# Placing the second halves of the value products on other columns of TensorE, in an attention and expert kernel

## The chip, the core and the metric

The program runs on one core of one Trainium2 chip, as one launch. The metric is the time of that launch on the device, in microseconds (us). Engines: TensorE (PE in the profile, PEld its weight loads), VectorE (DVE), ScalarE (ACT), GpSimd (POOL) and SyncE (SP), which issues the transfers. The engines run their own instruction streams in order and wait for each other on semaphores.

## What is computed

Attention over 4 batches of 12 heads (448 positions, 64 values each) with a soft cap on the scores, then a hidden layer with a squared ReLU, then a soft mixture of eight experts. Everything is float32.

```python
def _attn_ref(q, k, v, cap):                       # (4, 12, 448, 64)
    scores = cap * np.tanh(np.matmul(q, k.transpose(0, 1, 3, 2)) / np.sqrt(64) / cap)
    attn = np.exp(scores - np.max(scores, axis=-1, keepdims=True))
    attn = attn / (np.sum(attn, axis=-1, keepdims=True) + 1e-09)
    return np.matmul(attn, v)

def _moe_ref(x, w_in, w_out, s, b):                # 1792 tokens, 768 -> 2048 -> 768
    r = np.maximum(x @ w_in, 0.0)
    return (s * (r * r) + b) @ w_out

def _moe2_ref(x, phi, w1, w2):                     # 8 experts, 4 slots each
    ...
    d = softmax over tokens of x @ phi;  slot_input = d.T @ x
    for e in range(8): slot_out[e] = np.maximum(slot_input[e] @ w1[e], 0.0) @ w2[e]
    return softmax over slots of (x @ phi) @ slot_out
```

## The kernel before

**Groups, pairs, chunks.** The 48 heads are taken in twelve groups Q = 0 to 11 of four heads, three groups to a batch. A group is two pairs of heads (p = 2Q and 2Q+1), and i = 0 to 3 counts the heads of a group. The 448 key positions are cut in three chunks of 128 and a rest of 64 (c or k = 0 to 3, `KF` = 3 is the rest). Keys lie on the partitions of a score tile and queries along its free side. In a full chunk every head has a tile of 128 partitions. In the rest the two heads of a pair share one tile: the even head has partitions 0 to 63, the odd head 64 to 127 (`rows`, L186).

**Per group.** `scores` (L138) or, from Q = 6 on, `visit` (L162) makes the products of keys and queries, ScalarE takes tanh (L156, L158, L171, L180) and `expo` (L210) the exponential. `add` (L222) sums the chunks on VectorE into `es`, and `sums` (L232) sums `es` over the partitions with ones on TensorE; for Q < 3 the rests go straight into that sum (L240). ScalarE and VectorE then make its reciprocal `rec` (L243, L244).

**The value products.** `weighted` (L246) multiplies the exponentials by the values. Head i's 64 value columns are taken as two halves h of 32, so that each product uses 32 columns of TensorE and all four heads stand side by side in its 128 columns. The result `U` is one PSUM tile of 128 partitions and two banks; bank h holds half h, and head i has partitions 32i to 32i+31 in both. A chunk is therefore eight products of 448 columns: half 0 of heads 0 to 3, then half 1 of heads 0 to 3. In the rest a product has only 64 of the 128 rows of TensorE. Each float32 product is two weight loads and two matmuls in the trace. For Q < 3 the chunks are multiplied one by one; for Q = 3 to 5 chunks 0 and 1 together and later chunk 2 and the rest; from Q = 6 all 32 products in a row.

**The end of a group.** `finish` (L262) multiplies U by `rec` (L271), splits the outcome into a high part (L92, on ScalarE from Q = 2 on) and a low part (L93, on VectorE), and writes both into the tile x of the batch, whose layout `w_in` follows. U has one buffer, so that the next group's value products, and from Q = 6 on the second score tile of its first visit, wait until U has been read.

**The hidden layer.** For batch bi, `hidden` (L529) makes 16 blocks of 18 products (`hp`, L541) from x and the split `w_in` (`ws`, L525 and L526), then squares (L547, L548), and `post` and `chain` work the outcome into logits and slot inputs. Batch 0's block runs beside groups 3 to 5, batch 1's beside 6 to 8, batch 2's beside 9 to 11, batch 3's alone. Up to about the middle of the program VectorE and ScalarE also convert the weights from 64-bit patterns (`convert`, L388 to L421; results `wr` and `o`), which transfers bring in as `raw`. At the end 54 tiles of expert weights of 1 MB (`wt`) are streamed in for `tail`.

**The order.** A scheduler places the instructions of every engine from the program order, priorities and its own estimates of time, so that a change in one place can move instructions elsewhere. After it each engine runs its list in that order.

## Time and profile before

| | us |
|---|---|
| three runs | 620.32, 623.55, 622.86; median 622.86 |
| the profiled execution | 623.18 |
| its span, first to last instruction | 621.3 |
| TensorE busy | 573.0 |
| ScalarE busy | 400.4 |
| VectorE busy | 376.3 |
| TensorE clock granted, mean | 0.99 of 2.4 GHz |

The profiled execution's own time is 1.9 us above its span and 0.3 us above the median. Busy time is the time in which an engine had at least one instruction under way; side by side matmuls count once. The chain of waits is followed back from the last instruction, at each step to what released it. Times within the program are us from the span's start.

### The profile page before, as it was taken

The page shows a single profiled execution, that of the slowest core. Times are in us where ns is not written, and L with a number is a line of the kernel's source. Part 1 is how long each engine was busy: PE and PEld are TensorE (multiplying, and loading weights), DVE is VectorE, ACT ScalarE, POOL GpSimd, SP SyncE. Part 2 cuts the span into 40 slices and gives each one's busy share as a digit, 9 for nine tenths or more (in the row PEclk, how much of TensorE's full clock was granted, in tenths as well). Part 3 has the DMA queues.
Part 4 walks back from the last instruction along what each step waited for, and adds up shares of the span by engine and source line. Part 5 has one row for each costly group of instructions (what it writes and reads, how often), then busy time and mean ns, then how long its engine had stood idle before and what let it go on. Part 6 is the DMA issues. An engine that isn't in the chain of part 4 may idle for free.

```text
span 621.3 us, 11132 instructions
## 1 busy us (share of the span) xinstructions
PE 573.0 (92%) x4496; PEld 383.7 (62%) x4496; DVE 376.3 (61%) x557; ACT 400.4 (64%) x675; POOL 4.1 (1%) x11
## 2 busy tenths in 40 slices
PE   7898999999989999999999999999999998986662
PEld 5334565757667576575875675858788864345551
DVE  4999999999984868868739845452422224112221
ACT  5899788888769698497797694945456551001010
POOL 1000000000000000000000000000000000000000
PEclk8999999999999999999999999999999999999996
DMA  8844767777684662859755322115878859999997
GB/s 295 289 133 140 242 247 250 251 239 280 190 294 168 221 206 77 277 181 297 244 186 163 123 69 80 52 51 207 325 296 298 330 198 407 419 419 418 417 411 267
DMA packets 44875, 149.97 MB, mean 241 GB/s; under 512 B 4480, under 2 KB 18576, under 8 KB 37904
## 3 DMA queue, kind: packets, MB, share of 16 engines
q1 hardware_dynamic: 44528, 148.65, 66.6%
q8 instruction: 37, 0.61, 0.4%
q0 software_dynamic: 288, 0.53, 0.2%
q14 instruction: 22, 0.18, 0.1%
HBM read 131.07 MB, written 18.09 MB: 240 GB/s over the span
## 4 chain that ended last, share of the span: by engine, by line
PE 59%; DMA 14%; ACT 13%; DVE 9%; issue 3%; SPq 0%; DVEq 0%; ACTq 0%
PE hp L541 30%; DMA wt<-in_w_dram 12%; PE U L257 9%; PE tp L564 4%; ACT e L218 3%; ACT e L180 3%; PE sc L146 2%; PE pt L654 2%; PE sc L176 2%; PE L L578 2%; PE Sm L238 2%; ACT e L156 1%; ACT g L566 1%; DMA raw<-in_w_outT_dram 1%; ACT ws L525 1%
## 5 line engine op out<-in xcount | busy, mean ns | idle before, releaser
L541 PE MATMUL hp<-x,ws 128*128 128x448 f32 x1152 | 267.6, 375 | 0.0
L541 PEld LDWEIGHTS hp<-x,ws 128*128 128x128 f32 x1152 | 207.2, 188 | 43.4 <-issue 28.7
L526 DVE TENSOR_TENSOR ws<-wr,ws 128x384 fp32r<-128x384 f32 x128 | 70.0, 551 | 93.6 <-ACT ws L525 92.6
L525 ACT CAST ws<-wr 128x384 fp32r<-128x384 f32 x128 | 67.5, 532 | 40.9 <-PE hp L541 40.6
L257 PE MATMUL U<-e,v 128*32 128x448 f32 (+1 forms) x672 | 70.4, 548 | 3.3 <-ACT e L218 2.5
L218 ACT ACTIVATE e<-e,c_acap 128x1792 f32<-128x1792 f32 (+1 forms) x42 | 72.0, 1713 | 0.3
L566 ACT COPY g<-tp 112x256 f32<-112x256 f32 x128 | 44.2, 404 | 12.3 <-PE tp L564 11.5
L257 PEld LDWEIGHTS U<-e,v 128*32 128x32 f32 (+1 forms) x672 | 20.0, 110 | 42.8 <-issue 35.5
L156 ACT ACTIVATE e<-sc,c_tsc 128x896 f32<-128x896 f32 x36 | 35.5, 1005 | 11.1 <-PE sc L146 11.1
L564 PE MATMUL tp<-c_cst,r 128*112 128x128 f32 x256 | 39.3, 275 | 3.2 <-ACT g L566 2.4
L244 DVE RECIPROCAL rec<-rec 128x448 f32<-128x448 f32 x12 | 35.4, 2949 | 9.8 <-ACT rec L243 9.8
L910 ACT COPY wt<-op 128x512 f32<-128x512 f32 x12 | 7.0, 586 | 52.4 <-PE op L905 52.4
L547 ACT ACTIVATE r<-hp 128x448 f32<-128x448 f32 x63 | 35.4, 563 | 7.8 <-PE hp L541 7.8
L180 ACT ACTIVATE e<-sc,c_tsc 128x896 f32<-128x896 f32 x36 | 35.6, 1050 | 5.2 <-PE sc L176 5.2
L925 PE MATMUL so_ps<-wt,free 128*32 128x128 f32 x768 | 25.9, 275 | 13.7 <-DMA wt<-in_w_dram 13.7
L548 ACT ACTIVATE r<-r 128x448 f32<-128x448 f32 x63 | 38.1, 605 | 0.4
L564 PEld LDWEIGHTS tp<-c_cst,r 128*112 128x112 f32 x256 | 29.6, 133 | 12.9 <-ACT g L566 4.6
L388 ACT ACTIVATE o<-raw 128x768 f32<-128x768 f32 x32 | 29.9, 949 | 5.3 <-DMA raw<-in_w_outT_dram 3.7
L227 DVE TENSOR_TENSOR es<-e 128x1792 f32<-128x1792 f32 x12 | 24.3, 2026 | 12.7 <-ACT e L218 12.7
L925 PEld LDWEIGHTS so_ps<-wt,free 128*32 128x32 f32 x768 | 19.9, 109 | 18.1 <-DMA wt<-in_w_dram 15.6
L417 DVE SCALAR_TENSOR_TENSOR o<-raw,o 128x768 int32<-128x768 int32 x32 | 30.5, 954 | 0.3
L421 DVE SCALAR_TENSOR_TENSOR o<-raw,o 128x768 int32<-128x768 int32 x32 | 30.4, 953 | 0.2
(177 smaller groups left out, 675.2 us busy)
## 6 DMA issues: line engine op xcount, KB each, us to landing
wt<-in_w_dram SPq DMA_DIRECT2D x48, 1024.0 KB, 18.0
wr<-wsc SPq DMA_DIRECT2D x48, 384.0 KB, 3.5
raw<-in_w_in_dram SPq DMA_DIRECT2D x16, 768.0 KB, 5.5
raw<-in_w_outT_dram SPq DMA_DIRECT2D x16, 768.0 KB, 5.1
raw<-in_w_out_dram SPq DMA_DIRECT2D x16, 768.0 KB, 5.9
wsc<-wr SPq DMA_DIRECT2D x16, 384.0 KB, 2.7
osc<-o SPq DMA_DIRECT2D x16, 384.0 KB, 3.5
wt<-osc SPq DMA_DIRECT2D x6, 1024.0 KB, 6.9
```

Of the source, the lines that this page charges most:

```text
L156: nc.scalar.activation(self.e[Q][c][:, 2 * j:2 * j + 2, :], sc[:, :, :S], AF.Tanh, scale=self.c["tsc"])
L180: nc.scalar.activation(self.e[Q][c][:, 2 * j:2 * j + 2, :], sc[j][:, :, :S], AF.Tanh, scale=self.c["tsc"])
L218: ins = self.nc.scalar.activation(e, e, AF.Exp, scale=self.c["acap"]).ins
L244: nc.vector.reciprocal(self.rec, self.rec)
L257: products.append(lambda k=k, h=h, i=i, d=d: nc.tensor.matmul(self.U[32 * i:32 * i + 32, h, :S], self.v[2 * Q + i // 2][self.rows(i, k), d ...
L525: self.nc.scalar.copy(hi, u)
L526: self.nc.vector.tensor_sub(lo, u, hi.bitcast(F32))
L541: nc.tensor.matmul(hp[:, :S], ws[kc // 3][:, w, kc % 3, :], x[:, s, kc, :], start=(k == 0), stop=(k == 3 * KC - 1))
L548: self.mark = nc.scalar.activation(r2, r2, AF.Square).ins
L564: self.nc.tensor.transpose(tp[:CP, q * P:(q + 1) * P], r2[:, q * CP:(q + 1) * CP], self.c["idn"])
L566: self.nc.scalar.copy(self.g[q][:CP, :, fc * P:(fc + 1) * P], tp[:CP, 2 * q * P:2 * (q + 1) * P].rearrange("p (a b) -> p a b", b=P))
L925: nc.tensor.matmul(so_ps[32 * e:32 * e + 32, G, :], ht[G][:, f, 32 * e:32 * e + 32], w2[f // 4][:, f % 4, e, :], start=(f == 0), stop=(f = ...
```

## The change

Five things, all of them about where a half of a head or a rest stands.

1. `weighted`: half 1 of head i goes to column strip i ^ 2, so the strips of the second half come in the order 2, 3, 0, 1. In bank 1 of U the heads stand in the order 2, 3, 0, 1.
2. `rows`: in the rests of the odd pairs the two heads swap rows, so that heads 0 and 3 of a group have rows 0 to 63 and heads 1 and 2 rows 64 to 127. With the first point the eight products of a rest are in eight different parts of TensorE, of 64 rows by 32 columns each; before, the two halves of a head shared one part. The key layout `kT` and the value layout `v` are made to fit on the host.
3. `add`: the two sums of the rests (L230) take heads 0 and 3, and 1 and 2.
4. `finish`: the one product of U and `rec` becomes three, 128 partitions by 448 for bank 0 and twice 64 partitions by 448 for bank 1, each with the other half of `rec`.
5. `w_in` is laid out on the host so that its rows follow the new order of x. Sizes and counts of transfers are as before.

```diff
--- before.py
+++ after.py
@@ -185,7 +185,7 @@
 
     def rows(self, g, c):
 
-        return slice(0, P) if c < KF else slice(64 * (g % 2), 64 * (g % 2) + 64)
+        return slice(0, P) if c < KF else slice(64 * ((g ^ g // 2) % 2), 64 * ((g ^ g // 2) % 2) + 64)
 
     def greatest(self, g):
         nc, c = self.nc, self.c
@@ -227,7 +227,8 @@
                 self.nc.vector.tensor_add(es, e[0] if c == 1 else es, e[c])
             for i in range(2) if c == KF else ():
                 r = self.rows(i, c)
-                self.nc.vector.tensor_add(es[r, i::2, :], es[r, i::2, :], e[c][r])
+                j = slice(1, 3) if i else slice(0, 4, 3)
+                self.nc.vector.tensor_add(es[r, j, :], es[r, j, :], e[c][r])
 
     def sums(self, Q):
 
@@ -254,8 +255,9 @@
             for h in range(2):
                 for i in range(4):
                     d = (i % 2 * KF + k if k < KF else 2 * KF) * D + 32 * h
-                    products.append(lambda k=k, h=h, i=i, d=d: nc.tensor.matmul(
-                        self.U[32 * i:32 * i + 32, h, :S], self.v[2 * Q + i // 2][self.rows(i, k), d:d + 32], self.chunk(4 * Q + i, k),
+                    j = 32 * (i ^ 2 * h)
+                    products.append(lambda k=k, h=h, i=i, j=j, d=d: nc.tensor.matmul(
+                        self.U[j:j + 32, h, :S], self.v[2 * Q + i // 2][self.rows(i, k), d:d + 32], self.chunk(4 * Q + i, k),
                         start=(k == 0), stop=(k == KF)))
         self.together(products, Q >= 3)
 
@@ -268,7 +270,9 @@
         u = self.U[:, :, :S]
         out = self.c["hh"][:, :, :S] if Q < 2 else u
         with self.tc.high_priority(100) if Q < NQ else nullcontext():
-            nc.vector.tensor_mul(out, u, self.rec[:, None, :].to_broadcast([P, 2, S]))
+            nc.vector.tensor_mul(out[:, 0], u[:, 0], self.rec)
+            for a, b in ((0, 64), (64, 0)):
+                nc.vector.tensor_mul(out[a:a + 64, 1], u[a:a + 64, 1], self.rec[b:b + 64])
             self.split(hi, lo, out, Q < 2)
         del self.e[Q], self.v[2 * Q], self.v[2 * Q + 1]
 
@@ -1011,14 +1015,19 @@
     kt = np.zeros((B * NP, 2, D, KW), np.float32)
     kt[..., :n] = kd[..., :n].reshape(B * NP, 2, D, P, KF).swapaxes(3, 4).reshape(B * NP, 2, D, n)
     for i in range(2):
-        kt[:, i, :, n + 64 * i:n + 64 * i + 64] = kd[:, i, :, n:]
+        for j in range(2):
+            r = n + 64 * (i ^ j)
+            kt[j::2, i, :, r:r + 64] = kd[j::2, i, :, n:]
     a["kT"] = kt.reshape(B * NP, P, KW)
-    a["v"] = cc(np.concatenate([vd[:, i, :n].reshape(B * NP, P, KF * D) for i in range(2)] + [vd[:, :, n:].reshape(B * NP, P, D)], axis=2))
+    vr = vd[:, :, n:].copy()
+    vr[1::2] = vr[1::2, ::-1]
+    a["v"] = cc(np.concatenate([vd[:, i, :n].reshape(B * NP, P, KF * D) for i in range(2)] + [vr.reshape(B * NP, P, D)], axis=2))
     wi, wo = cc(inputs["moe_w_in"]), cc(inputs["moe_w_out"])
     f64 = wi.dtype == np.float64
     if f64:
         wi, wo = wi.view(np.int64), wo.view(np.int64)
-    wi = wi.reshape(NQ, 4, 2, D // 2, FF).transpose(0, 2, 1, 3, 4)
+    wi = wi.reshape(NQ, 4, 2, D // 2, FF).transpose(0, 2, 1, 3, 4).copy()
+    wi[:, 1] = wi[:, 1][:, [2, 3, 0, 1]]
     a["w_in"] = cc(wi.reshape(KC, P, FC, P).transpose(2, 1, 0, 3)).reshape(FC, P, KC * P)
     a["w_outT"] = cc(wo.reshape(FF // U, U, 2, KC // 2, P).transpose(0, 2, 4, 3, 1)).reshape(FF // U, 2, P, CU)
     a["w_out"] = wo.reshape(FC, P, DM) if f64 else cc(wo.reshape(FC, P, 3, U).transpose(2, 1, 0, 3)).reshape(3, P, 4096)
```

The scheduler's lists change too. Three places follow; line numbers behind L235 are those of each version (L271 before is L273 and L275 after, L417 L421, L541 L545).

VectorE at the end of group 2, whose x is the last that batch 0's hidden layer waits for; `wr`, `o` and `ws` are weights under conversion, `ql` the low part of a query. Before:

```order
L244 RECIPROCAL rec<-rec 128x448
L479 COPY c_hh<-pf 128x64
L271 TENSOR_TENSOR U<-U,rec 128x2x448
L421 SCALAR_TENSOR_TENSOR wr<-raw,wr 128x768
L93 TENSOR_TENSOR ql<-q_648,qh 128x448
L93 TENSOR_TENSOR x_396<-U,x_396 128x896
```

After:

```order
L245 RECIPROCAL rec<-rec 128x448
L483 COPY c_hh<-pf 128x64
L273 TENSOR_TENSOR U<-U,rec 128x448
L425 SCALAR_TENSOR_TENSOR wr<-raw,wr 128x768
L275 TENSOR_TENSOR U<-U,rec 64x448
L93 TENSOR_TENSOR ql<-q_652,qh 128x448
L275 TENSOR_TENSOR U<-U,rec 64x448
L530 TENSOR_TENSOR ws<-wr,ws 128x384
L397 TENSOR_SCALAR o<-o 128x768
L421 SCALAR_TENSOR_TENSOR o<-raw,o 128x768
L93 TENSOR_TENSOR x_396<-U,x_396 128x896
```

The three parts of the product stand apart, and between the last of them and the low part of x three more instructions have come.

TensorE at the same place; the product that waits for ScalarE is the first that needs this x, and the one that waits for VectorE the first that needs its low part. Before:

```order
L541 MATMUL hp<-x_396,ws 128x448 x6
L146 MATMUL sc<-qh,kh 128x448 [waits Activation_49]
L146 MATMUL sc<-qh,kh 128x448
L146 MATMUL sc<-ql,kh 128x448 x2
L146 MATMUL sc<-qh,kl 128x448 x2
L541 MATMUL hp<-x_396,ws 128x448 [waits Activation_49]
L541 MATMUL hp<-x_396,ws 128x448 x3
L541 MATMUL hp<-x_396,ws 128x448 [waits DVE_49]
```

After:

```order
L545 MATMUL hp<-x_396,ws 128x448 x6
L146 MATMUL sc<-qh,kh 128x448 [waits Activation_49]
L146 MATMUL sc<-qh,kh 128x448
L146 MATMUL sc<-ql,kh 128x448 x2
L146 MATMUL sc<-qh,kl 128x448 x2
L545 MATMUL hp<-x_396,ws 128x448 [waits Activation_49]
L545 MATMUL hp<-x_396,ws 128x448 x3
L545 MATMUL hp<-x_396,ws 128x448 [waits DVE_49]
```

What stands ahead of the eight rows of after is another six `hp` products and six of scores, which in before came behind them; the first product that needs this x has moved back by those twelve.

VectorE from the first reading of U to the low part of x at the end of group 3, which frees U for group 4. Before:

```order
L271 TENSOR_TENSOR U<-U,rec 128x2x448
L526 TENSOR_TENSOR ws<-wr,ws 128x384
L393 TENSOR_SCALAR o<-o 128x768
L93 TENSOR_TENSOR ql<-q_982,qh 128x448
L417 SCALAR_TENSOR_TENSOR o<-raw,o 128x768
L93 TENSOR_TENSOR x_1051<-U,x_1051 128x896
```

After:

```order
L273 TENSOR_TENSOR U<-U,rec 128x448
L93 TENSOR_TENSOR kl<-k_989,kh 128x512
L530 TENSOR_TENSOR ws<-wr,ws 128x384
L275 TENSOR_TENSOR U<-U,rec 64x448
L397 TENSOR_SCALAR wr<-wr 128x768
L275 TENSOR_TENSOR U<-U,rec 64x448
L227 TENSOR_TENSOR es<-e 128x1792
L530 TENSOR_TENSOR ws<-wr,ws 128x384
L93 TENSOR_TENSOR x_1057<-U,x_1057 128x896
```

Ahead of these rows one `ws` stands between the reciprocal and the product in before, and six instructions in after (two `ws`, one L397, two L425, one L421); a sum of 1792 elements has come in before the low part of x.

TensorE where group 4's first value products wait for that U. Before:

```order
L541 MATMUL hp<-x_396,ws 128x448
L257 MATMUL U<-e,v 32x448 x16
L470 MATMUL pp<-o,c_misc 32x256 x6
L541 MATMUL hp<-x_396,ws 128x448 x6
L478 MATMUL pf<-c_cst,c_tmp 128x32 x2
```

After:

```order
L545 MATMUL hp<-x_396,ws 128x448 x2
L474 MATMUL pp<-o,c_misc 32x256 x6
L545 MATMUL hp<-x_396,ws 128x448 x6
L482 MATMUL pf<-c_cst,c_tmp 128x32 x2
L146 MATMUL sc<-qh,kh 128x448 x2
L146 MATMUL sc<-ql,kh 128x448 x2
L146 MATMUL sc<-qh,kl 128x448 x2
L545 MATMUL hp<-x_396,ws 128x448 x7
L259 MATMUL U<-e,v 32x448 x16
```

The value products have moved back behind six `pp`, the next thirteen `hp`, two `pf` and six score products. The transfers change places by a few, and GpSimd's list not at all.

## Rows read from the trace of the kernel before

**Rows 1.** Stretches: length, busy us by engine (instructions), TensorE clock, DMA share, GB/s.
```profile
8.00:66.00 58.00, 51.63 (x398) 21.93 (x400) 53.52 (x68) 50.65 (x54) 0.00 (x0) 0.97 0.65 222
81.00:180.00 99.00, 96.69 (x629) 64.42 (x629) 92.05 (x117) 84.27 (x138) 0.00 (x0) 1.00 0.70 242
180.00:420.00 240.00, 235.74 (x1593) 160.49 (x1591) 164.66 (x227) 187.12 (x321) 0.54 (x1) 1.00 0.50 163
505.00:621.00 116.00, 83.73 (x1272) 51.53 (x1270) 24.69 (x66) 14.26 (x29) 0.54 (x1) 0.96 0.97 393
```

**Rows 2.** The chain that ended last: start us, us, what.
```profile
205.98 6.29 PE U L257 x64
...
403.00 6.29 PE U L257 x64
```

**Rows 3.** Timeline, group 6's rest: start us, us, engine, line, operation, tiles, count, [idle before <-released by].
```profile
210.55 0.15 PEld L257 LDWEIGHTS U<-er,v 64*32 64x32 f32 x8 [0.73 <-ACT kh L92]
210.56 1.71 PE L257 MATMUL U<-er,v 64*32 64x448 f32 x16
...
210.96 0.13 PEld L257 LDWEIGHTS U<-er,v 64*32 64x32 f32 x4 [0.25 <-issue]
...
211.33 0.13 PEld L257 LDWEIGHTS U<-er,v 64*32 64x32 f32 x4 [0.25 <-issue]
```

**Rows 4.** Timeline, score products of two heads, 64 rows by 128 columns each.
```profile
65.93 0.36 PE L146 MATMUL sc<-ql,kh 64*128 64x448 f32 x2
...
66.12 0.37 PE L146 MATMUL sc<-qh,kl 64*128 64x448 f32 x2
```

**Rows 5.** Timeline of TensorE, group 0: rests of the sums (Sm), then of the values.
```profile
28.48 0.57 PE L240 MATMUL Sm<-e,c_ones 64*32 64x448 f32 x3
28.50 0.56 PE L257 MATMUL U<-e,v 64*32 64x448 f32 x1
28.88 0.55 PE L240 MATMUL Sm<-e,c_ones 64*32 64x448 f32 x3
```

**Rows 6.** Timeline, end of group 2: VectorE, and TensorE's loads that wait for x.
```profile
65.95 1.10 DVE L271 TENSOR_TENSOR U<-U,rec 128x896 f32<-128x896 f32 x1
...
66.96 0.95 DVE L421 SCALAR_TENSOR_TENSOR wr<-raw,wr 128x768 int32<-128x768 int32 x1
...
68.38 1.09 DVE L93 TENSOR_TENSOR x<-U,x 128x896 fp32r<-128x896 f32 x1
...
68.65 0.71 PEld L541 LDWEIGHTS hp<-x,ws 128*128 128x128 f32 x4 [0.30 <-ACT x L92]
```

**Rows 7.** Group by form, VectorE: count, busy us, mean ns of one, idle before.
```profile
L230 DVE TENSOR_TENSOR es<-es,er 64x896 f32<-64x896 f32 x12 | 13.0, 1085 | 4.7 <-ACT er L218 4.5
```

**Rows 8.** Timeline, end of group 3 on VectorE.
```profile
103.21 0.55 DVE L393 TENSOR_SCALAR o<-o 128x768 int32<-128x768 int32 x1
103.68 0.62 DVE L93 TENSOR_TENSOR ql<-q,qh 128x448 fp32r<-128x448 f32 x1
104.22 0.95 DVE L417 SCALAR_TENSOR_TENSOR o<-raw,o 128x768 int32<-128x768 int32 x1
105.09 1.08 DVE L93 TENSOR_TENSOR x<-U,x 128x896 fp32r<-128x896 f32 x1
...
108.03 2.02 DVE L227 TENSOR_TENSOR es<-e 128x1792 f32<-128x1792 f32 x1
```

**Rows 9.** Timeline of TensorE, group 4's first value products.
```profile
106.58 3.21 PE L257 MATMUL U<-e,v 128*32 128x448 f32 x32
109.61 1.03 PE L470 MATMUL pp<-o,c_misc 128*32 128x256 f32 x12
110.58 1.48 PE L541 MATMUL hp<-x,ws 128*128 128x448 f32 x6
```

**Rows 10.** Timeline, end of group 4 on VectorE, group 5's first value products on TensorE.
```profile
137.67 0.55 DVE L526 TENSOR_TENSOR ws<-wr,ws 128x384 fp32r<-128x384 f32 x1
138.14 1.08 DVE L93 TENSOR_TENSOR x<-U,x 128x896 fp32r<-128x896 f32 x1
...
143.06 1.33 PE L257 MATMUL U<-e,v 128*32 128x448 f32 x12
```

## The prediction

> **What bounds the kernel now.** I read the stretches first, then the chain, then single products. In the stretches [rows 1] the reader is to see which engine is full where. From 8 to 66 us VectorE is busy 53.5 of 58 us and TensorE 51.6: VectorE, which converts weights, sets the pace. From 81 to 180 us TensorE is busy 96.7 of 99 and VectorE 92.1: TensorE binds, with VectorE close behind. From 180 to 420 us TensorE is busy 235.7 of 240, VectorE only 164.7 and ScalarE 187.1: TensorE alone binds. At the end, from 505 us, the transfers do (0.97 busy, 393 GB/s); they are not full before that, so what is gained or lost earlier should move this end along with it. The chain [rows 2] agrees: it goes through the value products of groups 6 to 11 on TensorE, six times L257 x64 of 6.29 us each. The granted clock is 0.97 to 1.00 of 2.4 GHz in all four stretches, so durations of one stretch can be used in another.
>
> **What a rest costs.** The rest of group 6 [rows 3] is 16 matmuls, two for each of its eight products, and takes four rounds: weight loads at 210.55 (eight, two to a part), 210.96 and 211.33 (four each). A round is 0.376 us, and four matmuls run in it, one per column strip. A product here uses 64 of the 128 rows, so half of TensorE stands still; both halves of a head share one part, and one waits for the other. That two row parts of the same columns can work at once is seen on the score products [rows 4]: two heads, rows 0 to 63 and 64 to 127, start together and the next two 0.19 us later.
>
> **The gain.** If the eight parts all work at once, a rest takes two rounds: 2 x 0.376 = 0.75 us less. There are twelve rests, 9.0 us on TensorE in all. The rests of groups 0 to 2 lie before 66 us, where VectorE sets the pace; I count nothing for them. The other nine lie in stretches where TensorE is 98% busy, and six of them on the chain: 9 x 0.75 = **-6.75 us**. Loads keep their count, and the first eight of 16 lie beside the matmuls already [rows 3]. The order 2, 3, 0, 1 of strips in full chunks leaves each strip with the same work; starts within a round are some 10 ns apart, so a change of order costs between 0 and 0.8 us over the program, taken as 0. The sums of the rests keep size and count (1085 ns each) [rows 7]; only the heads are chosen otherwise. Transfers keep their sizes, and what the host lays out costs no device time.
>
> **The price: three products in `finish`.** The one product of 896 elements occupies VectorE 1.01 us (65.95 to 66.96) [rows 6]. Three of 448 take its place. One of 448 elements occupies it 0.54 us (103.68 to 104.22) [rows 8], and 64 partitions take as long as 128 [rows 7], so 3 x 0.54 = 1.62: +0.61 us per group (by durations of single instructions, 3 x 0.62 against 1.10, +0.77). Nothing excludes that a 448-element product from PSUM is dearer than the one read from SBUF; the row of 896 with the same operands gives 0.55 for half, so I keep 0.6.
> - Groups 0 to 2: VectorE is full there, 3 x 0.61 = **+1.8 us** (0 if its 4.5 us of idle time take it, 2.3 at most).
> - End of group 2, whose x batch 0's hidden layer waits for: the order shows three products apart and three other instructions ahead of the low part. From the first product to the end of the low part: 0.54 + 0.87 + 0.54 + 0.54 + 0.54 + 0.47 + 0.47 + 0.87 + 1.09 = 5.9 us, with prices of [rows 8] and, for `ws`, 0.47 (137.67 to 138.14) [rows 10], against 3.5 (65.95 to 69.47) [rows 6]: 2.4 later, and 1.2 from the two finishes before, 3.6 in all. TensorE waited for this x already (0.30 us for the high part) [rows 6]. Its first product that needs it has moved back by six `hp` and six score products: six `hp` are about 1.3 us [rows 9], three score steps 0.6 [rows 4], 1.9 to 2.0. So 1.6 us of wait is new, of which 1.2 is the delay that is counted in the 1.8. The 0.4 left goes into the range.
> - End of group 3, which frees U for group 4: ahead of the low part of x stand, more than before, two `ws` (0.94), one L397 (0.47), two converts of 0.87 (1.74), the sum `es` (1.93 to 2.0) and the 0.61; with `kl` for `ql` this is 5.8 us later [rows 8, 10]. Group 4's value products started at 106.58 [rows 9], 0.41 after that low part had ended (105.09 + 1.08) [rows 8], and have moved back behind six `pp` (0.97), thirteen `hp` (2.8), three score steps (0.6) and two `pf` (0.3, as two `pp`): 4.7 us [rows 4, 9]. 5.8 - 4.7 - 0.4 = 0.7, and TensorE comes 0.75 earlier for the shorter rest of group 3: **+1.4 us** (0 to 2.5). What stands behind these products is then late as well, scores for ScalarE among them.
> - Groups 4 and 5: by the same prices U of group 4 comes free up to 5 us later, but that low part ended 3.8 us (139.22 to 143.06) before group 5's first value products [rows 10], which also move back behind eight `hp`, 1.6 us; 0, or 3.7 if that cover is gone. Group 5's x is due well after its end; 0.
> - Groups 6 to 11: VectorE has 75 us idle in 240 [rows 1], but x and U are on the way to the next group. 0 to 6 x 0.6 = 3.6; I take **+0.5**, since TensorE has score and hidden products to do while U is read.
>
> **The sum** against the profiled execution, 623.18 us (its span 621.3 and 1.9 outside; it is 0.3 above the median): 623.18 - 6.75 + 1.8 + 1.4 + 0.5 = **620.1 us**. About 0.5%, 3.1 us, is what a measurement of this kernel can tell from no change; the sum lies right at that bound (619.75 from the median).
>
> **Rivals.**
> - *Three rounds.* Each product is two matmuls of one part, one behind the other on TensorE's list. If a strip takes its matmuls in the order of the list, strip 0 first has both of head 0, then both of head 2: the second waits for the first, the third goes beside the second, the fourth follows. That is three rounds, and half the gain: 623.18 - 9 x 0.376 + 3.7 = **623.5**. For it: no row shows two row parts of one strip overtake each other, since the score products alternate on the list [rows 4]. Against it: in group 0 a value product starts at 28.50, ahead of three second matmuls of the sums at 28.88 which stand before it on the list [rows 5], so a blocked matmul does not hold up what is behind it in another strip. The Trainium skill ("TensorE: Matmul & The Clock Gate", Part 3, The mechanism) says that matmuls start and end strictly in program order, without reordering; by that, a second matmul that waits for its part would hold up all that follows. Between strips this case's trace disagrees (28.50 against 28.88); within a strip no run here shows it.
> - *No gain at all.* The parts don't work eight abreast, the change doesn't do what it says, and its price stays: 623.18 + 3.7 = **626.9**. Against it: in group 6's rest four parts of both row halves write the same bank in one round [rows 3], and two row parts with the same columns run at once into different banks [rows 4]; after the change only the number grows. The Trainium skill ("TensorEngine Tiling (Array Packing)", Gotcha 1: PSUM Pressure) says that different row tiles can't access the same PSUM bank at the same time; by that rule two of the four row-and-bank pairs would go at a time, four rounds as before and 626.9. The trace disagrees already before the change [rows 3].
> - *Slower by late x and U.* VectorE's thirds stand scattered among conversions, and all covers fail: 1.8 + 0.4 + 2.5 + 3.7 + 3.6 = 12.0 against 6.75: **628.4**. It happens where U and x are handed over in groups 2 to 11, and decides from 9.9 us of waits on (6.75 + 3.1). For it: VectorE is 93% busy from 81 to 180 us [rows 1]. Against it: TensorE's list has moved other work ahead of these waits.
> - *The price eats half.* Every group pays 0.6 on the chain and groups 2 to 4 somewhat more: 623.18 - 6.75 + 1.8 + 1.8 + 2.9 = **622.9**.
> - *The price is hidden.* VectorE's idle time takes it, and only the gain is left: **616.4** to 617.
>
> **Chances.** Forecast 0.43 (its own range 618 to 622; half of it beyond the bound), three rounds 0.20, no gain 0.07, slower by late x and U 0.10, price eats half 0.09, price hidden 0.11. Faster by over 0.5%: 0.22 of the forecast and 0.11 = 0.33. Within: 0.21 + 0.20 + 0.09 = 0.50. Slower: 0.07 + 0.10 = 0.17. The range reaches from the hidden price, 616.2, to no gain, 626.9; it leaves out the slower case and little else.
>
> **What would show it.** Gain: the 16 matmuls of a rest with loads in two groups of eight, 0.38 apart, in place of 8, 4 and 4; the chain's L257 x64 at about 5.5 us instead of 6.29. Three rounds: loads or starts at three times and about 5.9 us. No gain: 6.29. Price: products of `finish` at about 0.62 us each, also those of 64 partitions. Waits: new idle time of TensorE at the first `hp` of batch 0 (about 0.4 to 1.6 us) and before group 4's value products (about 1.4 us), none before group 5's. The prediction is wrong if TensorE's stretch from 180 to 420 us doesn't shrink by some 4 us (six rests), if new idle time on it eats that, or if the transfers at the end don't move along with it.

## The result and the profile after

| | median us, runs | ratio to before, 95% interval | mean granted clock of the runs |
|---|---|---|---|
| before | 623.06, 11 runs | 1 | 0.986 (104 runs, all batches) |
| the changed kernel | 630.86, 11 runs | 1.0116 [1.0092, 1.0139] | 0.976 |

By the ratio the changed kernel is 7.2 us slower (the medians differ by 7.8), where 3 us faster was forecast and 626.9 was the upper end. The profiled execution took 633.39 us, 2.5 above its median (that of before 623.18, about its median), so that the profiles show about 10 us of difference.

The rests do what was forecast. Timelines of TensorE's loads and matmuls for group 6's rest, after, columns as in [rows 3]:

```profile
221.37 0.18 PEld L259 LDWEIGHTS U<-er,v 64*32 64x32 f32 x16 [0.73 <-issue]
```

```profile
221.37 0.98 PE L259 MATMUL U<-er,v 64*32 64x448 f32 x16
```

All 16 loads come at once, and 16 matmuls take 0.98 us; before, it was loads of 8, 4 and 4 and 1.71 us. On the chain of waits, L259 x64 is now 5.56 us against 6.29 [rows 2]:

```profile
216.80 5.56 PE U L259 x64
...
416.48 5.56 PE U L259 x64
```

The stretches answer [rows 1]:

```profile
8.00:66.00 58.00, 46.37 (x344) 18.96 (x348) 48.87 (x64) 46.61 (x49) 0.00 (x0) 0.91 0.56 194
81.00:180.00 99.00, 94.69 (x640) 62.01 (x633) 94.93 (x122) 83.04 (x132) 0.00 (x0) 1.00 0.71 238
180.00:420.00 240.00, 229.03 (x1543) 156.27 (x1545) 168.95 (x238) 186.83 (x318) 0.54 (x1) 0.99 0.51 169
505.00:621.00 116.00, 95.44 (x1339) 62.31 (x1338) 26.38 (x69) 22.08 (x49) 0.54 (x1) 1.00 0.94 382
```

The reader is to see the first line: TensorE and VectorE are both less busy there than before (46.4 against 51.6 us, 48.9 against 53.5), and the granted clock is 0.91 against 0.97. In the third line TensorE is busy 229.0 of 240 us where it was 235.7. So the time went into waits, and into a lower clock.

**The first place** is the value products of group 2, which wait for U of group 1. Timeline of TensorE before, then all engines after:

```profile
51.18 3.21 PE L257 MATMUL U<-e,v 128*32 128x448 f32 x32 [0.73 <-DVE c_hh L271]
```

```profile
52.69 0.62 DVE L273 TENSOR_TENSOR c_hh<-U,rec 128x448 f32<-128x448 f32 x1
...
53.35 1.27 DVE L275 TENSOR_TENSOR c_hh<-U,rec 64x448 f32<-64x448 f32 x2
...
54.68 5.87 PE L259 MATMUL U<-e,v 128*32 128x448 f32 x32 [2.77 <-DVE c_hh L275]
```

TensorE waits 2.77 us where it waited 0.73, and the same 32 matmuls then take 5.87 us where they took 3.21. Both halves of the change lengthen this wait. With the separate parts alone and with the split of the product alone (`place_only` and `split_only_again`, both below) it is 1.51 and 1.92 us:

```profile
53.53 4.82 PE L259 MATMUL U<-e,v 128*32 128x448 f32 x32 [1.51 <-DVE c_hh L273]
```

```profile
52.66 4.78 PE L257 MATMUL U<-e,v 128*32 128x448 f32 x32 [1.92 <-DVE c_hh L273]
```

The shorter rests bring TensorE to the wait 0.8 us earlier, the split frees U 1.2 us later, and 0.73 + 0.8 + 1.2 = 2.7 (an estimate from these rows). Stretch 52 to 60 us of before, then of after:

```profile
52.00:60.00 8.00, 7.58 (x70) 3.20 (x62) 7.82 (x10) 7.66 (x10) 0.00 (x0) 1.00 0.13 36
```

```profile
52.00:60.00 8.00, 5.32 (x32) 1.38 (x32) 6.02 (x7) 4.38 (x4) 0.00 (x0) 0.58 0.25 95
```

The clock is at 0.58, most of the stretch at the lower of its two levels (1.2 GHz), and VectorE and ScalarE starve (6.0 and 4.4 us busy of 8). Group 2's reciprocal then starts 6.2 us later than before, and group 11's 12.8 us.

The table shows where each execution stands against the first profile of before: the start of VectorE's reciprocal of a group (in before at 63, 168, 214, 294, 344 and 411 us), and the end. The last column is an estimate of TensorE's time lost to the low clock: the trace in stretches of 4 us, (1 - clock) x 4, summed over those below 0.97, up to 516 us.

| us later than before | group 2 | 5 | 6 | 8 | 9 | 11 | end | low clock |
|---|---|---|---|---|---|---|---|---|
| before again | 0.4 | 0.0 | -0.1 | 0.4 | 0.4 | 0.4 | -1.9 | 0 (first profile 1.7) |
| after | 6.2 | 7.9 | 10.1 | 10.0 | 14.6 | 12.8 | 10.3 | 8.4 |
| after, 2nd | 4.6 | 3.8 | 4.7 | 7.2 | 10.6 | 9.2 | 9.6 | 5.1 |
| after, 3rd | 3.4 | 6.2 | 7.2 | 7.4 | 12.0 | 10.1 | 8.0 | 5.1 |
| split alone | 6.8 | 6.0 | 5.2 | 5.0 | 7.8 | 7.8 | 7.7 | 5.1 |
| split alone, 2nd | 3.1 | 2.3 | 1.5 | 1.5 | 4.5 | 4.5 | 3.8 | 1.7 |
| parts in groups 0 to 2 | 5.3 | 5.4 | 4.7 | 4.9 | 8.4 | 8.5 | 6.3 | 5.1 |
| parts in groups 3 to 11 | 3.3 | 3.6 | 5.4 | 5.5 | 9.2 | 7.8 | 5.5 | 5.1 |
| placement alone | 4.1 | 3.3 | 2.7 | 3.0 | 1.6 | 0.1 | -0.4 | 5.1 |
| late, product in SBUF | -0.1 | -0.4 | -1.9 | -2.6 | -3.9 | -6.0 | -8.0 | 0 |

Three losses stand out in the rows of the changed kernel: up to group 2; from group 5 to 6 (in the third profile also near 110 us); and from group 8 to 9. The second profile loses another 2.5 us from group 6 to 8. From group 9 to 11 all three win 0.7 to 0.95 us a group, the gain that was forecast.

### The profile page after: what moved, and what is told of

Its sections match the earlier page's. It is cut to its first block, busy times and chain, and to the rows that moved or that the text cites. A ratio compares the mean times of both kernels' runs of the same rounds, so it can differ in the third digit from the quotient of the medians.

```text
span 631.6 us, 11160 instructions
## 1 busy us (share of the span) xinstructions
PE 571.4 (90%) x4496; PEld 382.2 (61%) x4496; DVE 388.3 (61%) x581; ACT 401.7 (64%) x675; POOL 4.1 (1%) x11
## 4 chain that ended last, share of the span: by engine, by line
PE 49%; DMA 17%; DVE 14%; ACT 13%; issue 4%; SPq 1%; ACTq 0%; DVEq 0%
PE hp L545 26%; DMA wt<-in_w_dram 12%; PE U L259 6%; PE tp L568 3%; ACT e L218 3%; ACT e L180 2%; PE sc L176 2%; PE L L582 2%; DVE rec L245 2%; PE pt L658 2%; DMA osc<-o 2%; DMA raw<-in_w_in_dram 2%; ACT ws L529 1%; PE Sm L239 1%; DVE es L227 1%
## 5 line engine op out<-in xcount | busy, mean ns | idle before, releaser
L545 PE MATMUL hp<-x,ws 128*128 128x448 f32 x1152 | 271.2, 378 | 0.9 <-DVE x L93 0.9
L545 PEld LDWEIGHTS hp<-x,ws 128*128 128x128 f32 x1152 | 207.8, 189 | 46.8 <-issue 31.5
L259 PE MATMUL U<-e,v 128*32 128x448 f32 (+1 forms) x672 | 70.6, 570 | 8.3 <-ACT e L218 4.5
L259 PEld LDWEIGHTS U<-e,v 128*32 128x32 f32 (+1 forms) x672 | 19.5, 113 | 46.8 <-issue 34.3
L421 DVE SCALAR_TENSOR_TENSOR o<-raw,o 128x768 int32<-128x768 int32 x32 | 30.4, 952 | 0.3
L425 DVE SCALAR_TENSOR_TENSOR o<-raw,o 128x768 int32<-128x768 int32 x32 | 30.4, 951 | 0.3
```

Of the source, the lines that this page charges most:

```text
L259: products.append(lambda k=k, h=h, i=i, j=j, d=d: nc.tensor.matmul(self.U[j:j + 32, h, :S], self.v[2 * Q + i // 2][self.rows(i, k), d:d + ...
L545: nc.tensor.matmul(hp[:, :S], ws[kc // 3][:, w, kc % 3, :], x[:, s, kc, :], start=(k == 0), stop=(k == 3 * KC - 1))
```

## The experiments

Times are medians; ratios are to before in the same batch, and a difference in us is that ratio's, unless medians are named.

### The two halves of the change apart

Placement alone (`place_only`), against the changed kernel, with TensorE's list nearly that of before:

```diff
-            nc.vector.tensor_mul(out[:, 0], u[:, 0], self.rec)
-            for a, b in ((0, 64), (64, 0)):
-                nc.vector.tensor_mul(out[a:a + 64, 1], u[a:a + 64, 1], self.rec[b:b + 64])
+            nc.vector.tensor_mul(out, u, self.rec[:, None, :].to_broadcast([P, 2, S]))
```

> The changed kernel, but the end of a group is one product of U and rec again, so that half 1 of each head is divided by another head's sum (left out: the right divisor for bank 1). TensorE's list is almost that of the kernel before. Theory SPLIT (the three products in finish make the loss, the eight parts give 0.75 us in each of nine groups): 623.1 - 6.75 = 616.3 us (615 to 618.5). Theory PLACE (eight matmuls abreast cost time or clock elsewhere): about 628, as in the changed kernel less some DVE time. Theory ORDER (any edit moves the lists and the time by a per cent): within 1 us of 623 or anywhere from 617 to 630.

619.78 us, 0.9942 [0.9923, 0.9961]: 3.6 us faster. PLACE falls, the parts by themselves gain, though only about half of the 6.75 us that nine rests save.

The split alone (`split_only`), against before:

```diff
-            nc.vector.tensor_mul(out, u, self.rec[:, None, :].to_broadcast([P, 2, S]))
+            nc.vector.tensor_mul(out[:, 0], u[:, 0], self.rec)
+            for a in (0, 64):
+                nc.vector.tensor_mul(out[a:a + 64, 1], u[a:a + 64, 1], self.rec[a:a + 64])
```

> The kernel before, but with finish in three products (128 partitions by 448, then twice 64 by 448, each with its own heads' rec); no value product stands elsewhere. SPLIT: 623.1 + 7.8 + 6.75 = about 637.6 us (634 to 641). PLACE: 623 to 626, since the split alone costs VectorE 0.6 us a group. ORDER: the two parts don't add up, anything from 620 to 635.

627.58 us, 1.0071 [1.0049, 1.0092]: 4.4 us slower, not 14.5. The halves don't add up: -3.6 and +4.4 make +0.8, and the whole is +7.2. In its trace VectorE, ScalarE and GpSimd have the instructions of the changed kernel in the same order, row by row, and so has TensorE but for matmuls that run side by side. SyncE has not: three transfers stand elsewhere, two loads of `v` and one of `raw`. The expectation of `parts_from3`, below, takes the lists of all engines as the same. So the one of the two whose rests are 0.75 us shorter is 2.8 us slower, and the rests and the places of three transfers are both candidates for it.

The split in groups 0 and 1 alone (`split_first_two`, the same diff under `if Q < 2`), with the lists of TensorE and ScalarE as before:

> The kernel before, with finish in three products for groups 0 and 1 alone; the lists of TensorE and ScalarE are those of the kernel before. In the trace of the changed kernel TensorE is idle for 2.77 us ahead of group 2's value products (0.73 before) and these then run at half the clock (5.87 us in place of 3.21). Theory CLOCK (the late hand-over of U in group 1 drops the clock, which costs 2.7 us on top): 623.1 + 1.5 + 2.7 = 626 to 628 with the half clock in that stretch. Theory SMALL (0.6 to 0.8 us for each of two groups, the clock falls by chance): 623.5 to 625.

625.33 us, 1.0044 [1.0021, 1.0067], so +2.7. Between the two theories: in the profiled execution the wait ahead of group 2 is 1.90 us and the clock stays at 1.00, with 0.8 and 0.7 us lost in the two groups (SMALL); the other eleven executions lie between 1.9 us below and 4.2 us above it.

The split in groups 6 to 11 alone (`split_late`, `if Q >= 6`):

> The kernel before with finish in three products for groups 6 to 11 alone, every head's half where it was. ScalarE's list has the conversion ahead of group 9's first tanh, as in the changed kernel. Theory LIST with a small price: about 2 to 3 us lost between group 8's and group 9's reciprocal, under 0.2 us in each of the other groups: 625 to 627. Theory PRICE (0.5 to 0.6 us a group on the chain): 626 to 628 with steps of 0.5 in every group. Neither: 622.5 to 624.

626.31 us, 1.0043 [1.0021, 1.0064]. Its profile is of its longest execution, 629.12 us, and 1.8 us of the delay stand there ahead of group 6, where nothing was changed. From there the delay grows by 3.6 us from group 8 to 9, by 1.0 from group 5 to 6, and by no more than 0.4 in any other group: the products themselves are hidden in these groups, and LIST holds by the place of the loss. Timeline of ScalarE in before, in the changed kernel, and in this one, at group 9's first scores:

```profile
312.88 1.91 ACT L180 ACTIVATE e<-sc,c_tsc 128x896 f32<-128x896 f32 x2 [0.64 <-PE sc L176]
```

```profile
324.82 0.91 ACT L392 ACTIVATE o<-raw 128x768 f32<-128x768 f32 x1 [2.79 <-DMA osc<-o]
325.64 1.89 ACT L180 ACTIVATE e<-sc,c_tsc 128x896 f32<-128x896 f32 x2
```

```profile
317.80 0.90 ACT L393 ACTIVATE o<-raw 128x768 f32<-128x768 f32 x1 [2.62 <-DMA osc<-o]
318.59 1.90 ACT L180 ACTIVATE e<-sc,c_tsc 128x896 f32<-128x896 f32 x2
```

A conversion, for which the scheduler found an earlier place, stands ahead of the tanh and waits for the store of an older slice; scores that are ready wait behind it. SyncE's list of this stretch, which holds these stores, differs from that of before as well.

### Low clock, lists, or the parts

`before_again` and `after_again`, second profiles, and `after_third`:

> The kernel before, a second profile. Theory CLOCK (half clock follows from long waits of TensorE, by its place in the program): at most one stretch at 1.2 GHz within the first 30 us, some 2 us lost, none around group 2's value products or later. Theory CHANCE (the half clock comes and goes with the execution): other stretches than in the first profile.

> The changed kernel, a second profile. CLOCK: group 2's value products (x32, near 54 us) run at half the clock again behind a wait of over 2 us, and about 8 us in all are lost to half clock. CHANCE: the stretches are others, and the time goes with their sum.

> The changed kernel, a third profile: 5 to 8 us lost to half clock (8.4 and 5.1 in two), group 2's value products at half clock again behind a wait of over 2 us; span less this loss 623 to 626.

621.25, 632.66 and 631.08 us. Ahead of group 2's value products the changed kernel waits 2.77, 2.79 and 2.80 us in its three profiles and has the low clock behind it in all three (0.58, 0.61 and 0.79 from 52 to 60 us); before waits 0.73 twice and keeps 1.00. So that place is systematic. The other stretches at low clock differ from one execution to the next.

`after_fill`, products without use in TensorE's early waits:

```diff
+        n = {(0, 1): 6, (0, 2): 5, (1, 0): 3, (2, 0): 10}.get((Q, chunks[0]), 0)
+        ...
+                for _ in range(n):
+                    last = nc.tensor.matmul(w[:, :P], self.c["ones"], self.c["ones"], start=True, stop=True)
```

> The changed kernel with products that nobody reads (ones by ones, 128 columns) in four waits of TensorE: 6 ahead of group 0's second and 5 ahead of its third chunk, 3 ahead of group 1's and 10 ahead of group 2's value products; they fill 0.6 to 2.1 us each and the waits stay as long. CLOCK: the stretches at half clock up to 62 us are gone, which cost about 6 us in the profile of the changed kernel: 624 to 626 us. Theory WAIT (the waits themselves are the loss, the clock is a bystander): 630 to 632.

629.09 us, 1.0077 [1.0048, 1.0107]. The low clock up to 62 us is gone, though TensorE still waits 1.81 us there, and 2.4 us are won of the 5 to 6 expected: the time lies between the ranges of the two theories, and its interval overlaps that of the changed kernel. The wait is 1.0 us shorter too, so that not all of the 2.4 need be the clock's. Stretch 52 to 60 us:

```profile
52.00:60.00 8.00, 7.08 (x60) 2.78 (x60) 6.69 (x9) 4.64 (x7) 0.00 (x0) 1.00 0.07 28
```

`conv_behind`, the conversion behind group 9's tanh, and `after_both`, that and the fill:

```diff
-                with self.tc.issue_after(self.mark) if n == 4 and self.mark else nullcontext():
+                with self.tc.issue_after(self.mark) if n == 4 and self.mark else self.tc.issue_after(self.tanh) if n == 41 and self.tanh else nullcontext():
```

> The changed kernel with one instruction's place fixed: on ScalarE's list the conversion that stands ahead of group 9's first tanh (it waits there for a store of the one two before, 2.79 us idle in the changed kernel's profile, ending at 324.82) comes behind those two tanh, as in the kernel before. Theory LIST (this conversion delays group 9's scores by 2 to 3 us, and the half clock near 350 follows from it): 630.5 - 2 to 4 = 626.5 to 628.5, and from group 8's to group 9's reciprocal no more is lost (4.7 and 3.4 us in two profiles of the changed kernel). Theory SPLIT alone (the late hand-over of U and x): 629.5 to 631.

> The changed kernel with both: the products that fill TensorE's early waits, and the conversion behind group 9's tanh. If the two causes are separate their gains add up: 629.1 - 2 to 4 = 625 to 627. If both only shift where the same time is lost: 628.5 to 629.5.

`conv_behind`: 630.61 us, 1.0124 [1.0081, 1.0167], no gain by time. In its trace the step from group 8 to 9 is -0.2 us (it was +4.7, +3.4 and +4.6), as LIST said, but 3.0 are lost from group 9 to 10. Two conversions now wait there for a store, much longer than the one did ahead of the tanh; timeline of ScalarE:

```profile
356.74 1.70 ACT L395 ACTIVATE o<-raw 128x768 f32<-128x768 f32 x2 [6.20 <-DMA osc<-o]
```

`after_both`: 627.03 us, 1.0058 [1.0031, 1.0084], half of the loss. Its profile has no stretch at low clock up to 516 us, and this execution, 626.44 us, is still 3.3 us longer than the profiled one of before, which has 1.7 us of low clock. So what is left of the loss there isn't lost to the clock. What the conversion costs by itself in the changed kernel these two don't settle; the whole loss of `split_late` is 2.7.

`parts_from3` and `parts_to3`, the changed kernel with the parts in some groups only:

```diff
-                    j = 32 * (i ^ 2 * h)
+                    j = 32 * (i ^ 2 * h if Q >= 3 else i)
```

> The changed kernel with the separate parts for groups 3 to 11 alone; in groups 0 to 2 both halves of a head share a part again and a rest takes four rounds (left out: the order of w_in's rows for batch 0, whose values come out wrong). Finish is in three products everywhere, and the lists of all engines are those of the changed kernel and of the kernel with the split alone (627.6 us). Theory EARLY (the shorter rests of groups 0 to 2 make TensorE wait longer and lose its clock there, which is why the changed kernel is 3 us slower than the split alone): 627.6 - 9 x 0.3 to 0.75 = 621 to 625. Theory LATER (the loss of the separate parts lies in groups 3 to 11): 629 to 631.

> The complement: separate parts for groups 0 to 2 alone, four rounds in groups 3 to 11 (left out: the right order of w_in's rows for batches 1 to 3). Finish in three products everywhere. EARLY: the split alone and 2 to 3 us for the clock, 629.5 to 631. LATER: 626.5 to 628.

> The split alone, a second profile, for its stretches at half clock: 5.1 us were lost to them in the first one. If the separate parts lower the clock, about 4 to 5 us here against 5 to 8 in the changed kernel, and without them both stand at 624.

`parts_from3` 630.71 us, 1.013 [1.0093, 1.0167], as slow as the changed kernel; `parts_to3` 628.16 us, 1.0069 [1.0039, 1.01], as the split alone; `split_only_again` 626.88. EARLY, my own favourite, falls: what the changed kernel loses against the split alone, it loses in groups 3 to 11. The table says where: from group 5 to 6 `parts_from3` loses 1.8 us, while `parts_to3` and the split alone win 0.7. From group 6 to 11, where six shorter rests should win 4.5 us, its delay grows by 2.4, only 0.2 to 1.4 us less than in the other three profiles. Timelines of TensorE there, of the split alone and of `parts_from3`:

```profile
178.78 3.65 PE L543 MATMUL hp<-x,ws 128*128 128x448 f32 x17
182.36 1.06 PE L472 MATMUL pp<-o,c_misc 128*32 128x256 f32 x12
```

```profile
177.83 1.57 PE L549 MATMUL hp<-x,ws 128*128 128x448 f32 x7
181.84 1.06 PE L478 MATMUL pp<-o,c_misc 128*32 128x256 f32 x12 [2.44 <-DVE o L429]
```

And the stretch from 180 to 190 us of the same two:

```profile
180.00:190.00 10.00, 10.00 (x65) 7.74 (x64) 9.66 (x16) 7.61 (x17) 0.00 (x0) 1.00 0.88 328
```

```profile
180.00:190.00 10.00, 8.16 (x45) 6.80 (x47) 9.06 (x15) 6.18 (x14) 0.00 (x0) 0.83 0.64 243
```

`parts_from3` waits 2.44 us for VectorE's conversion, where the split alone arrives with no wait. The wait eats the gain of groups 3 to 5, and in this execution the low clock behind it (0.83) adds to it. In the changed kernel the wait at this `pp` is 2.92, 2.91 and 2.97 us. Two of these three profiles keep a clock of 1.00 from 180 to 190 us and lose 0.9 and 1.0 us from group 5 to 6 all the same. Before the change TensorE waited here too, 1.82 us, for a square on ScalarE. TensorE, before and in the changed kernel:

```profile
179.16 1.06 PE L470 MATMUL pp<-o,c_misc 128*32 128x256 f32 x12 [1.82 <-ACT r L547]
```

```profile
186.61 1.92 PE L474 MATMUL pp<-o,c_misc 128*32 128x256 f32 x12 [2.92 <-DVE o L425]
```

The wait that ends last there is neither VectorE's nor ScalarE's but that for a transfer: VectorE's conversion waits for ScalarE's, and ScalarE's for a load of `w_outT`; in before the square stands behind the same conversion. Timelines of ScalarE of before, the split alone and `parts_from3`:

```profile
173.86 0.89 ACT L388 ACTIVATE o<-raw 128x768 f32<-128x768 f32 x1 [3.47 <-DMA raw<-in_w_outT_dram]
```

```profile
177.63 0.91 ACT L390 ACTIVATE o<-raw 128x768 f32<-128x768 f32 x1 [0.29 <-DMA raw<-in_w_outT_dram]
```

```profile
177.35 0.89 ACT L396 ACTIVATE o<-raw 128x768 f32<-128x768 f32 x1 [3.04 <-DMA raw<-in_w_outT_dram]
```

SyncE issues a load of `v` ahead of that load in before, in `parts_from3` and in the changed kernel; in the split alone and in `parts_to3` it comes behind. Timelines of SyncE, of the split alone and of `parts_from3`:

```profile
172.09 0.42 SPq L384 DMA_DIRECT2D raw<-in_w_outT_dram  x1
...
183.05 1.04 SPq L117 DMA_DIRECT2D v<-in_v_dram  x2
```

```profile
169.26 0.33 SPq L117 DMA_DIRECT2D v<-in_v_dram  x1
...
170.11 0.43 SPq L390 DMA_DIRECT2D raw<-in_w_outT_dram  x1
```

From the issue of the load to the start of the conversion it is 5.5 us in the split alone and 7.2 us in `parts_from3`. So `parts_from3` and `parts_to3` differ in their rests and in the order of transfers, and which of the two makes the wait is not shown: no run moves the transfers alone.

In the third profile of the changed kernel there is another wait, near 110 us: ScalarE waits for a conversion of VectorE's, and TensorE for ScalarE (timelines of both):

```profile
108.29 0.90 ACT L392 ACTIVATE wr<-raw 128x768 f32<-128x768 f32 x1 [2.69 <-DVE o L425]
...
110.61 0.47 PE L146 MATMUL sc<-qh,kh 64*128 64x448 f32 x2 [2.96 <-ACT e L156]
```

`in_a_row`, the three products in one block of the scheduler:

```diff
+            with self.tc.tile_critical():
```

> The changed kernel with the three products of finish held together in one block, so that no other instruction of VectorE stands between them; x and U come up to 2.4 us earlier from group 2 on, while groups 0 and 1 are as they were. Theory SCATTER (the instructions between the thirds make the loss): 619 to 624. Theory SPLIT by length alone or by the clock in groups 0 and 1: 628 to 631.

688.27 us, 1.105. It tells nothing of the thirds: the block itself waits for transfers that its products don't need, and TensorE for the block.

```profile
36.82 0.62 DVE L274 TENSOR_TENSOR c_hh<-U,rec 128x448 f32<-128x448 f32 x1 [2.65 <-DMA k<-in_kT_dram]
...
38.95 5.53 PE L259 MATMUL U<-e,v 128*32 128x448 f32 x32 [4.37 <-DVEq L273]
```

### Versions that keep the gain

`late`: the change for groups 6 to 11 alone, where VectorE doesn't set the pace; the weight loads of batches 2 and 3 swap the rows. `late_fill`: with useless products in early waits.

```diff
+                self.nc.sync.dma_start(d[:, :, 0], w[:, :, 0])
+                for r in (0, 64):
+                    self.nc.sync.dma_start(d[r:r + 64, :, 1], w[64 - r:128 - r, :, 1])
```

> The change made for groups 6 to 11 alone; groups 0 to 5 are as before, and the weight loads of batches 2 and 3 swap rows (three transfers of the same bytes for one). Nothing changes up to 180 us, where VectorE and the clock bind. Theory SPLIT with CLOCK (the loss lies in the early groups): 6 x 0.75 = 4.5 gained, 6 x 0 to 0.6 given back by the three products: 619 to 621.5. Theory PLACE or ORDER: 623 to 627.

> The change for groups 6 to 11 alone, with products that nobody reads in TensorE's early waits (3 and 6 ahead of group 0's second and third chunk, 1 ahead of group 1's, 3 ahead of group 2's value products). Theory CLOCK: the stretch at half clock that the kernel before has in some executions (1.7 us in one of two profiles) is gone: 620.0 to 621.5, a little under the 621.6 without the fill. If the clock in the early part is no loss on average: 621.5 to 622.5.

621.62 us, 0.9975 [0.9957, 0.9994], and 621.91 us, 0.9972 [0.9949, 0.9995]: both a little faster than before, the fill without effect, as there is no long wait to fill (0.73 us ahead of group 2's value products in `late`). In both, group 10's scores wait for the low part of x, which frees U; timeline of TensorE in `late`:

```profile
388.63 0.47 PE L176 MATMUL sc<-qh,kl 64*128 64x448 f32 x2 [1.37 <-DVE x L93]
```

`late_sbuf` and `before_sbuf`: the products go into SBUF, so that U is free before x is made.

```diff
-        out = self.c["hh"][:, :, :S] if Q < 2 else u
+        out = self.c["hh"][:, :, :S] if Q < 2 else u if Q < 6 else self.e[Q][2][:, :2, :]
```

> The change for groups 6 to 11 alone, and in these groups finish writes the products of U and rec into SBUF (over the exponentials of chunk 2, which are read by then) in place of over U. U is then free when the last of the three products is through and not only behind the low part of x, some 2 to 3 us earlier, and the three products stand in a row. Theory HANDOVER (what is left of the price in groups 6 to 11 is U's late hand-over, 1.4 us ahead of group 10's scores in the profiles of late): 618.5 to 620.5, below the 621.6 to 621.9 of late. If U's hand-over has slack in the other groups and the lists move otherwise: 621 to 623.

> The kernel before with that step alone: groups 6 to 11 write the product of U and rec into SBUF, as one product; nothing else is changed. HANDOVER with no wait for U in the kernel before: 622.5 to 623.5, no change. If an earlier U helps the kernel before as well: 621 to 622.5, and the gain of late_sbuf over this one is that of the separate parts, 2 to 3 us.

`late_sbuf`: 618.13 us, 0.9897 [0.9860, 0.9933], faster than both kernels. `before_sbuf`: 622.72 us, 0.9978 [0.9952, 1.0005], not to be told from before. The time is that of HANDOVER: with U free early, the parts bring 4.6 us by the medians in these six groups (4.5 by the rests), in the table -0.4 at group 5 and -6.0 at group 11. The three products stand in a row, and no scores wait for x any more; in `late` three such waits make 2.2 us (0.43, 0.39 and 1.37). The other 2.7 of the 4.9 us between `late` and `late_sbuf` aren't traced to a wait. The lists of VectorE, ScalarE, TensorE and SyncE differ between the two, and that a luckier order makes part of the gain is not excluded. End of group 9 in `late_sbuf`:

```profile
377.04 0.61 DVE L280 TENSOR_TENSOR e<-U,rec 128x448 f32<-128x448 f32 x1
377.68 1.27 DVE L282 TENSOR_TENSOR e<-U,rec 64x448 f32<-64x448 f32 x2
...
379.46 0.19 PEld L176 LDWEIGHTS sc<-qh,kl 64*128 64x128 f32 x2 [0.17 <-issue]
```

## Why the prediction was wrong

- **The rest, 2 x 0.376 us a group: right.** 1.71 to 0.98 us and 6.29 to 5.56 on the chain. The rival of three rounds falls: the two matmuls of head 0 and the two of head 2 stand behind one another in strip 0's list, and all four parts of both are through in two rounds. The Trainium skill ("TensorE: Matmul & The Clock Gate", Part 3, The mechanism) says that matmuls start and end strictly in program order. Within a strip, too, the trace disagrees: 16 matmuls in 0.98 us.
- **The products, 0.62 us each, 64 partitions as dear as 128: right** (0.62, and 1.27 for two). In groups 6 to 11 they are hidden in `split_late`; with the shorter rests of `late`, 2.2 us of waits for x show, where 0.5 was taken.
- **"Durations of one stretch can be used in another", since the clock was 0.97 to 1.00 (the last stretch of [rows 1] has 0.96): the step that failed first.** A wait was priced at its own length. At group 2 the wait grew by 2.0 us, and 32 matmuls grew by 2.7 behind it. By the runs the split in groups 0 and 1 costs 2.7 us, where 1.2 of the 1.8 us fall to these two groups. But the clock is not the whole loss: the mean clock of all runs is 0.986 in before, 0.976 in the changed kernel and 0.977 in `parts_from3`, yet 0.985 in the split alone, which is 4.4 us slower, and 0.986 in `after_both`, which is 3.6 us slower. (These means also count the end of the program, where the transfers set the pace.)
- **Nine rests "in stretches where TensorE is 98% busy": the step that cost most of the gain.** From 81 to 180 us TensorE was the busier engine [rows 1], yet `pp` waited there before the change already, 1.82 us, behind a conversion that itself waited 3.47 us for a load. Busy time said that TensorE has little to spare, not that it sets the pace. The gain of groups 3 to 5 went into that wait, 2.91 to 2.97 us after the change: +0.9 to +2.2 us from group 5 to 6 where -0.7 was due, with the clock at 1.00 behind two of the three waits. From group 5 to 11, where six rests of 0.75 us were due, the delay grew by 4.9, 5.4 and 3.9 us.
- **ScalarE's list was not looked at.** I followed VectorE and TensorE through the moved instructions. In the second half the largest loss, 3.4 to 4.7 us from group 8 to 9, stands at a conversion on ScalarE that moved ahead of a tanh. It was priced at nothing. Moving it back alone won nothing either (`conv_behind`).
- **"Transfers keep their sizes": their order was priced at nothing.** The waits near 180 us and from group 8 to 9 both end in a transfer, a load (3.53 us in the changed kernel) and a store (2.79 us), and SyncE's list had moved in both places.
- **Group 3's x and U, +1.4: not seen.** From group 2 to 5 the three profiles give +1.6, -0.8 and +2.9 us, where -0.9 was forecast; the spread is that of the waits on conversions.
- **The end moves along: right within 2.5 us**, the delay at group 11 (12.8, 9.2, 10.1) being that of the end (10.3, 9.6, 8.0).
- The rival "slower by late x and U" had the sign and the place, but neither the clock nor ScalarE's and SyncE's lists, and its condition, covers that fail at every hand-over, isn't what happened.

What stays open: how the 7.2 us divide. The early waits with their clock give 2.4 (`after_fill`), the conversion up to 2.7 (`split_late`), the parts, or the order of transfers that came with them, 2.8 against the split (`split_only` and the changed kernel). These were measured in different settings, and removing one cause moved part of the loss elsewhere (`conv_behind`). That the clock makes most of it is not shown. `after_fill` comes nearest to keeping the waits and changing the clock, and wins a third of the loss; `after_both`, whose profile has no low clock up to 516 us, keeps half of it.

## What to carry to other kernels

Making the busiest engine's work shorter pays only where it isn't waiting for another; elsewhere it lengthens a wait, and on TensorE a longer wait can cost its own length again in clock (here 2.0 us of wait and 2.7 us behind it). Before counting a gain, look for the wait that ends last in that stretch, on every engine's list, also those of engines that the change doesn't touch and of the transfers. Where a step adds instructions at a hand-over, free the handed-over buffer first, and use the step only where the added instructions are hidden: the same change was +1.2% everywhere, -0.3% in six groups alone, and -1.0% there with the buffer freed first.

## What the runs showed of the hardware

- The same wait is followed by the low clock in some executions and not in others. Ahead of group 2's value products, waits of 0.72 to 0.74 us left the clock at 1.00 in all six profiles that have them. Of ten with 1.5 to 2.8 us and no useless products ahead, eight had it low (0.57 to 0.79 in 52 to 60 us), while 1.90 and 2.04 kept 1.00. At the `pp` near 180 us 1.82 us kept it twice (before) and 1.83 lost it (`late`), 2.92 lost it and 2.91 and 2.97 kept it (the changed kernel). The Trainium skill ("TensorE: Matmul & The Clock Gate", Part 1, What's actually happening) says that the same kernel has different numbers of slow products from run to run. The traces agree: behind waits of 2.77, 2.79 and 2.80 us the same 32 products of the changed kernel take 5.87, 5.64 and 4.91 us.
- With useless products issued ahead of it, a wait of 1.81 us kept the clock at 1.00 in both profiles that have it (`after_fill`, `after_both`). Without them 1.90 us kept it once and 1.90 and 1.92 us lost it (`split_first_two`, `split_only` and its second profile); two profiles against three are few.
- Eight matmuls of 64 rows by 32 columns, from both halves of the rows and into two banks, run abreast: 16 take 0.98 us, where four at a time took 1.71 us.
